# Block merges of a chunked recurrence on one engine, a new block layout, and a new instruction order

## The chip, the cores and the metric

One core of a Trainium2 chip runs the kernel. The time is device microseconds (us) of one execution. A core has a matrix engine (TensorE, PE in the profile, with its weight loads as PEld), VectorE (DVE), ScalarE (ACT) and GpSimd (POOL); SyncE (SP) issues most of the DMA transfers. Each engine takes its instructions in the order in which the program lists them, and waits where an operand is not there yet.

## The reference

Part one is a linear recurrence over 768 steps for 4 batches and 8 heads with a 40x40 state; part two is a two-layer mixer on its output.

```python
for t in range(768):                                   # state: [4, 8, 40, 40]
    y[:, :, t] = einsum('bhd,bhde->bhe', r[t], state)
    Sa = einsum('bhde,bhe->bhd', state, a[t])
    state = state * w[t][:, :, None, :] - einsum('bhd,bhe->bhde', Sa, b[t])
    state = state + einsum('bhd,bhe->bhde', v[t], k[t])
x = y.transpose(0, 2, 1, 3).reshape(4, 768, 320)
h = maximum(x.transpose(0, 2, 1) @ w_tok1, 0) @ w_tok2  # 768 -> 256 -> 768
u = x + h.transpose(0, 2, 1)
out = u + maximum(u @ w_ch1, 0) @ w_ch2                 # 320 -> 1536 -> 320
```

## The kernel before

The 768 steps of a batch are cut into 12 chunks of 64, so there are 48 chunks (number 0 to 47), taken one after the other: the state passes from chunk to chunk in the chain (`t_chain`, the lines from 1236 on). What a chunk needs besides the state is prepared ahead. Sixteen chunks are a *unit* (three units); `t_prep` takes a unit in four quarters of 128 partitions each: running products of w by a scan (L550), a reciprocal (L564, L583), then RC, a product of eight steps, each on the result of the one before (L577 for the first, L579 for seven more; `prc` is the name of its tile in the odd quarters of unit 0), and two multiplies of the inputs by RC (L422, `pin<-pin,RC`) and one by the products themselves. The results go to DRAM (`sKB`, `sA`, `sP`) and come back chunk by chunk. P is the part of that product by which a chunk's y is multiplied in the end.

Inside a chunk of 64 steps the rank-one terms are coupled by a triangular 64x64 system. Its two 32x32 diagonal blocks are inverted for a *set* of eight chunks at once on VectorE (`t_solve`, six sets): ScalarE or VectorE copies the blocks out of TensorE's result into the tile `Dg` (`e3` in `t_a`, L886 and L890), one transpose turns them (L930, into `DT`), 15 pairs of multiply and reduce invert the 16x16 blocks (L952, L954), and *left* and *right* steps (L967 and L969, L988, L980 and L983) merge 16-blocks into 32-blocks. Two more transposes give TBt and TBn (L1008, L1013). For the first `pem` sets the left and right steps are left out, and TensorE merges the 16-blocks instead, chunk pair by chunk pair: `merge`, with 64 matmuls of 32x32 (L1102), a half copy (L1109) and two adds (L1114) on VectorE for each chunk, and an additional copy `noff` (L875) of the off-diagonal block. From TBt and TBn, `t_b` makes the 64-blocks (TensorE L1155, L1180, L1205), and the chain of a chunk can begin: `pq` (L1271), a copy (L1286), a second product (L1291), and RM on VectorE (L1327 in the first chunks, later L1321), which marks a chunk's start in what follows.

`t_y` multiplies the chunk pair's y by P: P comes by a DMA on SyncE's queue (L1435, `UB<-sP`), the multiply is L1437. The mixer (`t_mlp`) runs batch by batch beside the recurrence of the next batches, and after chunk 47 alone for the last batch; its weights are split in two parts ahead (`t_piece`, tiles `cv_t`, `cv_c`).

The order of all this isn't written by hand. Each stage is a Python generator that yields its instructions; a `Planner` builds the list of each engine from them at compile time, by ranks (when a piece is due) and by assumed costs. All ranks and choices stand in one table of numbers, `K`. Where the planner expects TensorE to stand still, it puts in *filler* matmuls (L409, 128x192 on constants, with a result that nobody reads), from `fill` us on.

Of the kernel before, what the change touches and what calls it, by code (L numbers as in the profile page):

```python
# [26 lines left out]
K = dict(mgs=0, mgl=0, lat=[200.0, 150.0, 145.0, 90.0], aff=[1.42609, 1.1641], affx=[1.5189, 1.1228], aff_g=8.09865,  # L27
         sets=[8, 8, 8, 8, 8, 8], atn=6, kbp=2, ld=6.86684, ldk=0.75246, v=10.13755, vg='APD', tbd_early=39.49165,
         tbd=[['DP', 'AD', 'DP', 'AP'], ['DA', 'PD', 'PD', 'P']], alt_c=1, slack=-25499.24339, evm=32.40994,
         slack_c=220.65128, p_rc=[1, 0, 1], p_a=[0, 0, 0], p_k=[0, 0, 0], solve=[3.58374, 3.18399, 3.06635, -7.44996,  # L30
         3.58843, -8.1416], solve_span=16.42651, atomic=0, a=11.69153, a_span=3.813, b=1.3893, chain=0.36562,
         evac=12.39546, y=-0.34229, utr=-4.08779, pem=1, mrg=2.46972, ea=7.45819, prp=15, psp=10, w=3, c=2, m=2,
         warm=0, fill=6, fill_cols=9045.48295, prep=[-24.70881, 2.11658, 24.34216], prep_step=[2.30023, -1.32604,
         0.5187], p_wg=[1, 3], p_big=[2], mlp=[11.83919, 26.61413, 33.74329, 43.48104], mlp_span=[14.28446, 11.00328,
         12.73272, 15.91023], conv_t=4.92844, conv_t_span=1.14477, conv_c=3.69813, conv_c_span=11.72512, conv_after=4,
         e_k=-29.62124, e_a=-24.52265, e_s=-2.04992, e_x=-24.28583, e_l=-10.57978)
# [1988 lines left out]
```

## Time and profile before

| | us |
|---|---|
| median of 3 runs (863.05 to 863.92) | 863.5 |
| the profiled execution | 866.96 |
| its span in the trace | 865.3 |
| TensorE busy | 785.6 (91%) |
| VectorE busy | 603.2 (70%) |
| ScalarE busy | 411.0 (47%) |
| GpSimd busy | 188.5 (22%) |

The busy shares are averages over three stages: up to about 115 us there is preparation only and no chunk runs; then the chunks run, with more and more of the mixer beside them; from about 790 us on only the last batch's mixer is left. TensorE's share holds 84.5 us of filler matmuls. A time in the trace is counted from the span's start.

### The profile page before, as it was taken

Reading aid. Unit: us, or ns where it says so; the run is one execution under the profiler, and the core shown is the slowest. Engines: PE = TensorE matmul, PEld = TensorE weight load, DVE = VectorE, ACT = ScalarE, POOL = GpSimd, SP = SyncE. Lnnn points to the kernel's source line nnn. Section 1 sums busy time; section 2 is a strip of 40 time slices with the busy share of each in tenths; the row PEclk is TensorE's granted clock in tenths of the full one; section 3 lists DMA queues with packets and bytes.
Section 4 is the critical chain, followed back from the end, with each engine's and each line's share of the span. In section 5 each row is a group of like instructions: output and inputs, shape, how many; then the busy total and the mean of one; then the engine's idle time right before and its main releaser. Section 6 shows DMA issues by size and latency. Waiting matters only on the chain.

```text
span 865.3 us, 31442 instructions
## 1 busy us (share of the span) xinstructions
PE 785.6 (91%) x13365; PEld 689.9 (80%) x13365; DVE 603.2 (70%) x1450; ACT 411.0 (47%) x1136; POOL 188.5 (22%) x314
## 2 busy tenths in 40 slices
PE   5798898888987979897999999999999999999997
PEld 4697786777876867786787988888888888989997
DVE  5657489999889969899663799438975444535332
ACT  2444365457767645447554655454453333423111
POOL 7500222234436123214420110111120001000000
PEclk7889788778978869998899999999999999999999
DMA  8489157998879866866958754743745445335341
GB/s 321 167 160 231 46 175 219 239 261 196 243 185 268 289 168 205 225 142 170 242 143 254 185 147 114 180 94 86 222 127 165 128 115 152 116 108 188 101 147 49
DMA packets 191379, 150.86 MB, mean 174 GB/s; under 512 B 147200, under 2 KB 167424, under 8 KB 188160
## 3 DMA queue, kind: packets, MB, share of 16 engines
q1 hardware_dynamic: 184896, 101.59, 45.6%
q0 software_dynamic: 6336, 47.19, 17.0%
q8 instruction: 107, 1.75, 0.9%
q14 instruction: 40, 0.33, 0.1%
HBM read 114.34 MB, written 34.41 MB: 172 GB/s over the span
## 4 chain that ended last, share of the span: by engine, by line
PE 47%; DVE 14%; issue 11%; DMA 9%; ACT 3%; POOL 1%; SPq 0%; ACTq 0%; POOLq 0%; DVEq 0%
PE m L1673 14%; PE m L1783 10%; DMA cv_c<-in_moe_w_ch_dram 3%; PE ph L1205 3%; PE yb L409 2%; DMA wg_t<-sT 2%; PE pq L1291 2%; DMA sG<-cv_c 2%; PE pq L1271 2%; PE pq L1296 2%; PE yb L1412 2%; PE px L845 1%; PE pU L298 1%; PE pt L1180 1%; DMA UB<-sP 1%
## 5 line engine op out<-in xcount | busy, mean ns | idle before, releaser
L1783 PE MATMUL m<-ut,wg_c 128*128 128x384 f32 x768 | 164.3, 351 | 0.6 <-DVE hd L1796 0.6
L1673 PE MATMUL m<-wg_c,hd 128*128 128x320 f32 x864 | 150.2, 318 | 1.9 <-DVE hd L1796 1.9
L1673 PEld LDWEIGHTS m<-wg_c,hd 128*128 128x128 f32 x864 | 129.8, 189 | 6.5 <-DVE hd L1796 3.6
L1783 PEld LDWEIGHTS m<-ut,wg_c 128*128 128x128 f32 x768 | 130.6, 190 | 5.5 <-DVE hd L1796 0.8
L1794 ACT ACTIVATE hd<-m 128x384 fp32r<-128x384 f32 x96 | 47.2, 491 | 136.5 <-PE m L1783 135.4
L1824 DVE TENSOR_TENSOR x<-m,x 128x320 f32<-128x320 f32 x96 | 46.8, 488 | 65.0 <-PE m L1673 64.6
L1796 DVE SCALAR_TENSOR_TENSOR hd<-m,hd 128x384 fp32r<-128x384 f32 x96 | 53.3, 555 | 50.4 <-ACT hd L1794 49.7
L409 PE MATMUL yb<-ident 128*128 128x192 bf16 x664 | 84.5, 272 | 3.0 <-POOL ident masks.py:199 1.7
L409 PEld LDWEIGHTS <-ident 128*128 128x128 bf16 x664 | 61.8, 108 | 15.1 <-issue 6.8
L422 POOL TENSOR_TENSOR cv_c<-cv_c 128x384 f32<-128x384 f32 (+3 forms) x48 | 49.0, 1021 | 83.1 <-DVE cv_c L1506 31.8
L886 ACT ACTIVATE Dg<-px 128x128 f32<-128x128 f32 (+1 forms) x135 | 52.9, 392 | 29.6 <-PE px L845 19.5
L1146 POOL COPY TBD<-TBt 32x256 f32<-32x256 f32 x43 | 31.3, 729 | 117.8 <-PE ph L1205 66.7
L1386 ACT COPY STs<-pU 40x160 f32<-40x160 f32 x88 | 25.0, 284 | 65.9 <-PE pU L298 64.6
L1608 POOL DMA_DIRECT2D wg_c<-sG x32 | 17.8, 557 | 166.9 <-PE m L1783 72.3
L1412 PE MATMUL yb<-KB,RM 128*64 128x40 f32 x768 | 39.4, 226 | 1.2 <-issue 1.2
L1271 PE MATMUL pq<-RV 40*64 40x64 f32 x768 | 37.6, 233 | 2.3 <-issue 1.5
L1305 POOL TENSOR_TENSOR RM<-UB,upp 64x128 f32<-64x128 f32 x30 | 15.6, 526 | 107.4 <-ACT UB L1286 98.0
L1271 PEld LDWEIGHTS pq<-RV 40*64 40x64 f32 x768 | 30.7, 143 | 10.0 <-issue 7.5
L1291 PE MATMUL pq<-UB 104*64 104x104 f32 x240 | 33.8, 311 | 3.6 <-ACT UB L1286 3.6
L1286 ACT COPY UB<-pq 104x256 f32<-104x256 f32 x96 | 31.5, 378 | 11.8 <-PE pq L1271 11.2
L298 PE MATMUL pU<-id,UB 40*40 40x40 f32 x352 | 24.7, 205 | 13.5 <-DVE UB L1371 8.8
L1412 PEld LDWEIGHTS yb<-KB,RM 128*64 128x64 f32 x768 | 34.1, 141 | 3.0 <-issue 2.7
(200 smaller groups left out, 1755.4 us busy)
## 6 DMA issues: line engine op xcount, KB each, us to landing
wg_c<-sG POOLq DMA_DIRECT2D x16, 1152.0 KB, 6.4
wg_c<-sG POOLq DMA_DIRECT2D x16, 960.0 KB, 5.4
pin<-in_wakb_dram SPq DMA_DIRECT2D x12, 960.0 KB
wg_t<-sT POOLq DMA_DIRECT2D x8, 1280.0 KB, 7.0
RV<-in_rvt_dram SPq DMA_DIRECT2D x48, 208.0 KB
sKB<-pin SPq DMA_DIRECT2D x12, 640.0 KB
KB<-sKB SPq DMA_DIRECT2D x48, 160.0 KB
KBp<-sKB SPq DMA_DIRECT2D x40, 160.0 KB
```

The source lines that it names most:

```text
L298: nc.tensor.matmul(out_, lhsT=in_, rhs=idn, start=True, stop=True, is_transpose=True)
L409: nc.tensor.matmul(yb[:, 320:512], lhsT=zf[:, 0:128], rhs=zf[:, 0:192], start=True, stop=True)
L422: return [(e, Port(60 + f * n / 0.96 if e == "DVE" else 140 + 2.24 * n), lambda e=e: engines[e].tensor_tensor(out=out_(), in0=a_(), in1=b_ ...
L886: act_ = ("ACT", 395, lambda: nc.scalar.activation(out=o_, in_=i_, func=AF.Copy, scale=-1.0))
L1271: nc.tensor.matmul(pqs[g][z][0][c0:c1, j, D:DP], lhsT=l_, rhs=rb[z * 64:z * 64 + D, j, :], start=True, stop=True)
L1291: nc.tensor.matmul(d["pq"][64:128, j, :], lhsT=hu[:, gi, j, :], rhs=hv(G)[:, j, :], start=True, stop=True)
L1412: nc.tensor.matmul(py[g - 1][z * 64:z * 64 + 64, h, :], lhsT=rms[g - 1 + z][:, h, :], rhs=o["kb"][:, h, :], start=h == 2 * j, stop=False)
L1673: nc.tensor.matmul(d[key], lhsT=lhs(i, a_), rhs=rhs(i, b_), start=i == 0 and j == 0, stop=i == n - 1 and j == 2)
L1783: nc.tensor.matmul(pt, lhsT=mm_[q][0], rhs=mm_[q][1], start=q == 0, stop=q == len(mm_) - 1)
L1794: nc.scalar.activation(out=hid[key][:, 0], in_=pt, func=AF.Relu)
L1796: now = yield [("DVE", dve(384), lambda: nc.vector.scalar_tensor_tensor(out=hid[key][:, 1], in0=pt, scalar=0.0, in1=hid[key][:, 0].bitcast ...
L1824: now = yield [("DVE", dve(320), lambda: tt(out=x()[:, i], in0=d[("c2", g, i)], in1=x()[:, i], op=ALU.add))]
```

## The change

Five things change, all in one edit of the table and a few lines of code.

1. `pem` goes from 1 to 0: the 16-blocks of all six sets, the first included, are merged by the left and right steps on VectorE. The `merge` work (512 small matmuls, 8 half copies, 16 adds, 8 `noff` copies) is no longer in the program.
2. `Dg` is stored chunk by chunk, so that the copies into it write whole rows, and the transpose L930 reads it with a stride.
3. The load of P is a small generator of its own, `pload`, with a due time ahead of the y matmuls; `t_y` is started by the main loop.
4. RC of unit 0 may go to VectorE or GpSimd (`p_rc` 2 for 1: the planner takes the one that is free by its count); RC of unit 1 goes to GpSimd (1 for 0).
5. All ranks of `K` and a few assumed costs have other numbers, and filler matmuls may stand from 2 us on, not 6. This gives another order on every engine. The program has 1217 filler matmuls, where it had 664.

Of the table, these two lines show the kind (the rest is numbers in the same manner):

```diff
-         slack_c=220.65128, p_rc=[1, 0, 1], p_a=[0, 0, 0], p_k=[0, 0, 0], solve=[3.58374, 3.18399, 3.06635, -7.44996,
+         slack_c=253.99266, p_rc=[2, 1, 1], p_a=[0, 0, 0], p_k=[0, 0, 0], solve=[5.34224, 2.30103, 3.06635, -9.75835,
-         evac=12.39546, y=-0.34229, utr=-4.08779, pem=1, mrg=2.46972, ea=7.45819, prp=15, psp=10, w=3, c=2, m=2,
+         evac=11.65466, y=0.17357, utr=-1.79783, pem=0, mrg=0.91121, ea=7.77917, prp=14, psp=10, w=3, c=2, m=2,
```

The code:

```diff
 # t_a, e3
-            o_, i_ = Dg[sl, :, ci * NP:(ci + 1) * NP].rearrange("p s n -> p n s"), pxb[sl, :, c0:c0 + L]
+            o_, i_ = Dg[sl, ci * NP:(ci + 1) * NP, :], pxb[sl, :, c0:c0 + L]
 # t_solve, first
-                nc.vector.transpose(out=d["DT"][:, 0:1024].rearrange("p (t s) -> p s t", t=L), in_=Dg)
+                nc.vector.transpose(out=d["DT"][:, 0:1024].rearrange("p (t s) -> p s t", t=L), in_=Dg.rearrange("p n s -> p s n"))
 # t_y
+        direct = bi == B - 1
+        pt = Pv_
+        p_ev = Event()
+
+        def pload():
+            yield g - K["y"] - K["y_ld"]
+            yield R_p
+            now = yield [("SP", (640.0, 960.0, 1024), lambda: nc.sync.dma_start(out=pt, in_=sP[u][:, cu - 1:cu + 1].rearrange("h c t e -> (c t) h e")))]
+            P.set(p_ev, now)
+        now = yield None
+        P.spawn(pload(), g - K["y"], now)
+        for z in range(2):
             for e in range(2):
                 yield rm_done[g - z][e]
...
-        direct = bi == B - 1
-        if not direct:
-            yield R_p
-        elif c == 1:
+        if direct and c == 1:
...
-        yield [("SP", (640.0, 960.0, 1024), lambda: nc.sync.dma_start(out=pt, in_=sP[u][:, cu - 1:cu + 1].rearrange("h c t e -> (c t) h e")))]
+        yield p_ev
         P.hold = 1e12
         now = yield [("DVE", dve(320), lambda: tt(out=to, in0=py[g - 1], in1=pt, op=ALU.mult))]
...
-            P.rel(R_p, now)
+        P.rel(R_p, now)
```

What it does to the order, at four places.

VectorE, the end of the first set's solve, before: the last pair of the 16-blocks, the two transposes, two products `AT` of chunks further on, and the half copies (`ET`) and adds of the merges on TensorE (`pm`).

```order
L952 TENSOR_TENSOR tmp_15_1160<-Tl_114,DT_954 128x450
L954 TENSOR_REDUCE Tl_114<-tmp_15_1160 128x2x15
L1008 STREAM_TRANSPOSE TBt_1183<-Tl_114 128x1024
L1013 STREAM_TRANSPOSE TBn_1210<-Tl_114 128x1024
L871 TENSOR_TENSOR AT_126<-px_1157,low_90 128x4x64
L871 TENSOR_TENSOR AT_126<-px_1158,low_91 128x4x64
L1109 TENSOR_SCALAR ET_135<-pm_1235,half 128x4x16
L1114 TENSOR_TENSOR TBt_1183<-pm_1235,TBt_1183 128x4x16
L1114 TENSOR_TENSOR TBn_1210<-pm_1235,TBn_1210 128x4x16
```

VectorE at the same place, now: after the last pair the left steps follow (`tmp_x`, `DT`) ...

```order
L954 TENSOR_REDUCE Tl_114<-tmp_14_1189 128x2x14
L952 TENSOR_TENSOR tmp_15_1207<-Tl_114,DT_1004 128x450
L954 TENSOR_REDUCE Tl_114<-tmp_15_1207 128x2x15
L967 TENSOR_TENSOR tmp_x_0_1232<-DT_1004,Tl_114 128x512
L969 TENSOR_REDUCE DT_1004<-tmp_x_0_1232 128x8x4
L967 TENSOR_TENSOR tmp_x_8_1255<-DT_1004,Tl_114 128x512
L969 TENSOR_REDUCE DT_1004<-tmp_x_8_1255 128x8x4
```

So the merge has moved from TensorE's results into VectorE's own list, ahead of the transposes, and these come 51 rows below that pair. Right ahead of them stand the last of nine steps on converted weights (`cv_t`), and behind them the multiply by RC of unit 1's second quarter, its scan, and the first copy `TBD` for a chunk's 64-blocks:

```order
L1515 SCALAR_TENSOR_TENSOR cv_t_0_128_1500<-cv_t_0_128_1500 128x384
L1515 SCALAR_TENSOR_TENSOR cv_t_0_0_1506<-cv_t_0_0_1506 128x384
L422 TENSOR_TENSOR cv_t_0_0_1506<-cv_t_0_0_1506 128x384
L1008 STREAM_TRANSPOSE TBt_1768<-Tl_114 128x1024
L1013 STREAM_TRANSPOSE TBn_1795<-Tl_114 128x1024
L422 TENSOR_TENSOR pin_1_1200<-pin_1_1200,RC_1_1663 128x640 x2
L544 COPY D_110<-CP_1_1595 128x40
L550 SCALAR_TENSOR_TENSOR CP_2_1851<-pin_2_993,D_110 128x680
L422 TENSOR_TENSOR pin_1_1200<-pin_1_1200 128x640
L1186 COPY TBD_156<-pt_1861 32x4x32
```

The copy `TBD`, too, now stands behind all this. Between the two places stand the left and right steps, mixed with the scans and reciprocals of unit 1's first two quarters and the multiplies of the first; these stood behind the merges before.

TensorE, ahead of the first chunk's 64-blocks (`pe`), before: the last matmuls of a merge, then `pe`.

```order
L298 MATMUL pk_0_1525<-ident,KBp_118 104x128 x4
L1102 MATMUL pm_1497<-ET_135,TBn_1210 32x32 x16
L1102 MATMUL pm_1497<-TBn_1210,ET_135 32x32 x16
L1155 MATMUL pe_1524<-TBt_1183,N_0_758 32x32
L1155 MATMUL pe_1524<-TBt_1183,N_1_770 32x32
```

TensorE now, at the same `pe` (`ident` and `yb` are a filler matmul's operands):

```order
L409 LDWEIGHTS ident
L409 MATMUL yb<-ident 128x192
L1155 MATMUL pe_1797<-TBt_1768,N_0_837 32x32
L1155 MATMUL pe_1797<-TBt_1768,N_1_844 32x32
L1155 MATMUL pe_1797<-TBt_1768,N_0_837 32x32
```

The merges are gone, and `pe` follows on filler matmuls, 172 in one piece. From the last `px` of the first set's chunks to this `pe` there are 443 of them in all (188 in the same stretch before).

SyncE's queue, the load of P for the chunk pair 16 and 17, before: it stands behind the two loads of unit 2's last quarter (`pin_3`) and a store of weights (`sG`).

```order
L509 DMA pin_3_5610<-in_wakb_dram 128x680
L1519 DMA sG_178<-cv_c_2_2_5378 128x384 x2
L509 DMA pin_3_5610<-in_wakb_dram 128x1920
L425 DMA RV_146<-in_rvt_dram 104x512
L1435 DMA UB<-sP_168 128x8x40
L425 DMA RV_147<-in_rvt_dram 104x512
L1057 DMA KB_5700<-sKB_162 128x8x40
L425 DMA W2s_145<-in_vtok_dram 64x320
```

Now (`pin_1` and `pin_2` are that unit's second and third quarter):

```order
L425 DMA W2s_143<-in_vtok_dram 64x320
L425 DMA sKB_163<-pin_1_4839 256x1x640
L425 DMA sA_166<-pin_1_4839 8x8x640 x2
L425 DMA sP_169<-pin_1_4839 128x640
L1406 DMA UB<-sP_168 128x8x40
L1057 DMA KB_5232<-sKB_162 128x8x40
L509 DMA pin_2_5318<-in_wakb_dram 128x680
L509 DMA pin_2_5318<-in_wakb_dram 128x1920
```

The load has moved ahead by a quarter of the unit: it stands behind the stores of the second quarter and ahead of the loads of the third.

## Rows read from the trace of the kernel before

**Rows 1.** The page: its first line, and shares of the chain that ended last.

```profile
span 865.3 us, 31442 instructions
...
PE 47%; DVE 14%; issue 11%; DMA 9%; ACT 3%; POOL 1%; SPq 0%; ACTq 0%; POOLq 0%; DVEq 0%
```

**Rows 2.** Windows: stretch, length, busy us of each engine (instructions), PE clock, DMA share.

```profile
64.40:115.30 50.90, 44.05 (x1043) 38.02 (x1040) 34.85 (x86) 24.11 (x61) 6.75 (x9) 0.87 0.54 146
...
115.30:221.50 106.20, 90.87 (x1973) 78.15 (x1972) 96.33 (x217) 62.86 (x164) 33.33 (x39) 0.81 0.85 222
...
404.00:431.00 27.00, 24.01 (x409) 19.66 (x409) 19.19 (x40) 15.73 (x43) 12.08 (x19) 0.75 0.91 225
...
431.00:790.00 359.00, 350.92 (x5604) 306.94 (x5602) 223.06 (x582) 165.74 (x497) 44.47 (x77) 1.00 0.54 147
```

**Rows 3.** Timeline of VectorE: start, length, line, operation; in brackets idle time before it.

```profile
16.01 1.56 DVE L422 TENSOR_TENSOR pin<-pin,RC 128x640 f32<-128x640 f32 x2 [6.36 <-POOL RC L579]
...
39.00 0.82 DVE L422 TENSOR_TENSOR pin<-pin,prc 128x640 f32<-128x640 f32 x1 [3.81 <-POOL prc L579]
...
64.37 1.97 DVE L930 STREAM_TRANSPOSE DT<-Dg 128x1024 f32<-128x1024 f32 x1 [0.20 <-ACT Dg L886]
...
79.58 1.21 DVE L1013 STREAM_TRANSPOSE TBn<-Tl 128x1024 f32<-128x1024 f32 x1
...
115.28 0.42 DVE L1327 TENSOR_TENSOR RM<-pq,upp 128x256 f32<-128x256 f32 x1
...
221.48 0.42 DVE L1327 TENSOR_TENSOR RM<-pq,upp 128x256 f32<-128x256 f32 x1 [1.31 <-ACT W2s L1337]
```

**Rows 4.** Timeline of GpSimd, 12 to 31 us: RC of the first unit.

```profile
12.76 3.21 POOL L579 TENSOR_TENSOR RC<-RC,pin 128x80 f32<-128x80 f32 x7
...
25.39 5.75 POOL L579 TENSOR_TENSOR RC<-RC,pin 128x80 f32<-128x80 f32 x7
```

**Rows 5.** VectorE by line: busy us, mean ns of one, then idle us before them.

```profile
L967 DVE TENSOR_TENSOR tmp_x<-DT,Tl 128x512 f32<-128x512 f32 (+2 forms) x30 | 21.3, 712 | 0.6
...
L980 DVE TENSOR_TENSOR tmp_y<-DT 128x512 f32<-128x512 f32 (+2 forms) x30 | 18.0, 600 | 0.5
...
L983 DVE TENSOR_REDUCE Tl<-tmp_y 128x32 f32<-128x384 f32 (+3 forms) x30 | 17.9, 595 | 0.6
...
L969 DVE TENSOR_REDUCE DT<-tmp_x 128x32 f32<-128x512 f32 (+3 forms) x30 | 17.8, 592 | 0.5
...
L579 DVE TENSOR_TENSOR RC<-RC,pin 128x80 f32<-128x80 f32 x28 | 11.3, 404 | 0.1
...
L550 DVE TENSOR_TENSOR_SCAN CP<-pin,D 128x680 f32<-128x680 f32 x10 | 16.4, 1643 | 1.6 <-DMA pin<-in_wakb_dram 1.3
...
L422 DVE TENSOR_TENSOR pin<-pin,RC 128x640 f32<-128x640 f32 x20 | 16.1, 819 | 7.2 <-POOL RC L579 7.0
...
L890 DVE TENSOR_SCALAR Dg<-px 32x128 f32<-32x128 f32 x9 | 3.7, 406 | 1.5 <-ACT Dg L886 1.4
...
L875 DVE TENSOR_SCALAR N<-px 128x128 f32<-128x128 f32 x8 | 2.3, 287 | 0.8 <-PE px L761 0.8
```

**Rows 6.** Timeline of TensorE between 66 and 102 us.

```profile
67.22 0.60 PE L298 MATMUL pk<-ident,KBp 128*104 128x128 f32 x4
...
67.66 2.97 PE L409 MATMUL yb<-ident 128*128 128x192 bf16 x34
...
94.39 5.01 PE L409 MATMUL yb<-ident 128*128 128x192 bf16 x36
...
101.40 0.21 PE L1155 MATMUL pe<-TBt,N 32*32 32x32 f32 x1
```

**Rows 7.** Windows for line L409 alone: the filler matmuls, from chunk 0 to 8.

```profile
115.30:221.50 106.20, 13.52 (x99) 9.53 (x99) 0.81 0.85 222
```

**Rows 8.** VectorE by line: the multiply with P.

```profile
L1437 DVE TENSOR_TENSOR UB<-yb,UB 128x320 f32<-128x320 f32 x18 | 8.7, 482 | 9.7 <-DMA KB<-sKB 5.0 <-DMA UB<-sP 4.5
...
L1437 DVE TENSOR_TENSOR x<-yb,UB 128x320 f32<-128x320 f32 x6 | 2.9, 490 | 5.8 <-DMA UB<-sP 5.8
```

More of the change, by code (lines that the diff above doesn't have):

```diff
@@ L24 @@
 LAT = {"PE": 190.0, "ACT": 210.0, "DVE": 130.0, "POOL": 150.0, "SP": 1000.0, "SWD": 1100.0}
[L27 to L36 removed]
+K = dict(mgs=0, mgl=0, lat=[200.0, 150.0, 145.0, 90.0], aff=[1.78829, 1.1641], affx=[1.45405, 1.4136], aff_g=9.17793,
+         sets=[8, 8, 8, 8, 8, 8], atn=6, kbp=2, ld=6.28181, ldk=0.00651, v=7.41899, vg='DAP', tbd_early=37.54021,
+         tbd=[['DP', 'AD', 'DP', 'PA'], ['DA', 'A', 'PD', 'PA']], alt_c=1, slack=-26924.458, evm=27.39028,
+         slack_c=253.99266, p_rc=[2, 1, 1], p_a=[0, 0, 0], p_k=[0, 0, 0], solve=[5.34224, 2.30103, 3.06635, -9.75835,
+         3.58843, -15.141], solve_span=15.10055, atomic=0, a=11.69153, a_span=3.89302, b=1.3893, chain=0.2847,
+         evac=11.65466, y=0.17357, utr=-1.79783, pem=0, mrg=0.91121, ea=7.77917, prp=14, psp=10, w=3, c=2, m=2,
+         warm=0, fill=2, fill_cols=9045.48295, prep=[-21.43568, -0.09764, 24.34216], prep_step=[2.31794, -1.32604,
+         0.31432], p_wg=[1, 3], p_big=[2], mlp=[11.83919, 26.61413, 33.74329, 43.92168], mlp_span=[14.28446, 11.00328,
+         12.73272, 15.91023], conv_t=5.1196, conv_t_span=-1.53208, conv_c=3.86709, conv_c_span=11.83065, conv_after=2,
+         y_ld=0.77206, e_k=-29.43179, e_a=-22.97064, e_s=-12.37189, e_x=-24.15062, e_l=-16.89014)
 class Port(float):
@@ L552, in scan @@
                         data1=D1.rearrange("p e t -> p (e t)"), initial=0.0, op0=ALU.mult, op1=ALU.add)
-                now = yield [("DVE", Port(120), carry), ("DVE", 1490, scan)]
+                now = yield [("DVE", Port(250), carry), ("DVE", 1560, scan)]
                 P.set(scan_ev[q], now)
@@ L559, in comp @@
                 cq = ce[:, q * n8:(q + 1) * n8]
-                yield [("ACT", 245, lambda: nc.scalar.activation(out=cq, in_=CPv[:, :, 7], func=AF.Square))]
+                yield [("ACT", 330, lambda: nc.scalar.activation(out=cq, in_=CPv[:, :, 7], func=AF.Square))]
                 def rec():
@@ L928, in first @@
                 d["DT"] = ap_.tile([128, 1056], F32, tag="t4", name=f"DT{i}", bufs=4)
-                nc.vector.transpose(out=d["DT"][:, 0:1024].rearrange("p (t s) -> p s t", t=L), in_=Dg)
-            now = yield [("DVE", 1810, first)]
+                nc.vector.transpose(out=d["DT"][:, 0:1024].rearrange("p (t s) -> p s t", t=L), in_=Dg.rearrange("p n s -> p s n"))
+            now = yield [("DVE", 2300, first)]
             P.set(Dg_free[i + 1], now)
@@ L1340, in body @@
             now = yield None
-            if c % 2 and gi:
-                P.spawn(t_y(g), g - K["y"], now)
             if last:
@@ L1878, in tile_kernel @@
                 P.spawn(t_b(g), g - K["b"])
+            else:
+                P.spawn(t_y(g), g - K["y"])
         for gi in range(2):
```

11 lines of the change are left out of this document (5 added, 6 removed).

## The prediction

> **What bounds the kernel now.** I read the page first: 865.3 us of span, and in the chain that ended last 47% TensorE, 14% VectorE, 11% issue and 9% DMA [rows 1]. Such shares mix stages, so the next view is the windows [rows 2]. The reader is to see two regimes. From 115.3 to 221.5 us VectorE is busy 96.33 of 106.2 us, TensorE 90.87, of which 13.52 are fillers [rows 2, 7]: VectorE is the engine that nothing can be taken from. From 431 to 790 TensorE is busy 350.92 of 359 us at a clock of 1.00, VectorE only 223.06: there the matrix work sets the pace. Before 115.3 no chunk runs; VectorE is busy 34.85 of the last 50.9 us of it. The third view is the timeline of VectorE [rows 3], for the points where stages begin: the first transpose at 64.37, TBn of the first set ending at 80.8, the first RM (chunk 0) at 115.28, RM of chunk 8 at 221.48. Chunk 8 is the first that needs the second set, whose solve shares VectorE with chunks 0 to 7. So an earlier end comes from an earlier chunk 8, if TensorE can use the time further on.
>
> The sum is made in the profiled execution, 866.96 us (its span and 1.66 around it). It lies 3.46 above the median of 863.5; I lay the difference on the median.
>
> **Up to the first transpose.** In the first quarter VectorE waits 6.36 us for RC, in the fourth 3.81 for prc [rows 3]. GpSimd's seven steps begin at 12.76 and take 3.21, beside a busy VectorE 5.75 [rows 4]. In the new order four of the first quarter's eight steps are VectorE's, then three GpSimd's, then one VectorE's. GpSimd still gets there at 12.76 only, so the gain is the half of its steps, 2 us. In the fourth quarter all eight are VectorE's: 8 x 0.404 = 3.2 us [rows 5] in place of GpSimd's chain and the wait; I count 3 us for that and for the second quarter, whose chain is shared now. Then the copies: eight `noff` copies go, 8 x 0.287 = 2.3 us by the N copies [rows 5]. VectorE's copy into Dg, a quarter of the N copy's partitions and the same row length, takes 406 ns against N's 287 [rows 5]; Dg is written with a stride and N in a row, so I take 287 for the new copies. VectorE has twelve of them (nine before), four on all partitions: 12 x 0.287 = 3.4 against 9 x 0.406 = 3.7, and ScalarE's, of which VectorE waits for several, shrink as well; 1.3 us in all. Sum 8.6, so the transpose starts near 56 instead of 64.37. Ends: nothing gained (64.4), and 10.2, the two whole waits, with it.
>
> **The first set's solve.** From the transpose to the end of TBn before: 16.4 us [rows 3]. To that come left and right: five sets took 21.3 + 18.0 + 17.9 + 17.8 = 75.0 us [rows 5], 15.0 a set. Among them stand 23 other rows: two scans (2 x 1.64), three multiplies (3 x 0.82) [rows 5], nine weight steps and some ten small ones, together 19 to 20 at 0.44, the mean of the window (96.33 us in 217) [rows 2]: 14.5 in all. TBn ends at 56 + 16.4 + 15.0 + 14.5 = 102. Instructions that stood behind the merges are ahead of TBt now, and a late one (RC of unit 1 comes from GpSimd, the weights by DMA) holds TBt, with every chunk behind it. The merges on TensorE, which go, ended so that `pe` ran at 101.40 [rows 6]. TensorE's queue has to be there as well: 443 fillers at 2.97 / 34 = 0.087 us [rows 6] are 38.7 us, twelve groups of small transposes 12 x 0.60 = 7.2 [rows 6], four groups of px a little more; begun at some 53 us (the last px of the set, an estimate: it has to be copied before the transpose at 56), that ends near 103. I take `pe` at 103.
>
> Dg is read with a stride by the transpose now. L930 with a strided side took 1.97 us, L1013 with none 1.21 [rows 3]. A second strided side costs between nothing and another 0.76; I take 0.75, since one side did: 1.5 us for the two transposes ahead of the first RM. The Trainium skill ("SBUF — State Buffer", section "Door 1: The DMA port swizzle") speaks against this part of the change: accesses that go to a new 16-byte line each time pay a penalty, so that a stride beyond four fp32 is not free. The rows with one strided side agree with that; by it the new transpose is dearer on both sides, and by a rule that only the worse side counts the sum would be 1.5 us smaller.
>
> From `pe` to the first RM it took 115.28 - 101.40 = 13.9 us before. So the first RM comes at 103 + 13.9 + 1.5 = 118.4, say 119: **3.7 us later** than before.
>
> **Chunk 0 to 8.** Counted in the two orders with the rows' durations, VectorE has 106.1 us of work between these RMs before, which is the stretch's length of 106.2, and 81.1 after. What goes: 24 steps of RC of unit 1, to GpSimd, 24 x 0.404 = 9.7; three scans (4.9) and eight multiplies (8 x 0.82 = 6.6), done ahead of chunk 0 now; reciprocals and small steps of the same, and the last half copies and adds of the merges, 17 at about 0.35, 6; against that 2 us of weight steps come in. The stretch can't be shorter than 81.1, if VectorE stays as full as before. TensorE without fillers needs 90.87 - 13.52 = 77.3. The DMA share is 0.85 [rows 2], so 0.85 x 106.2 = 90.3 us in which the DMA engines are at work; if all of that had to pass in the stretch, it would be the bound. Some of it is weights, which can come later. I take 87: **19.2 us less**.
>
> **From chunk 8 on.** The counted work of VectorE is the same from 8 to 16 (98.3 and 98.0) and 16 to 24 (98.3 and 96.1), and the mixer's matmuls stand beside the same chunks from 33 on. The shift is carried, with one exception: around chunks 22 and 23 the new order has 98 fillers more, 98 x 0.087 = 8.6 us in which the planner saw TensorE without work, and there (404 to 431) the clock was 0.75 and the DMA share 0.91 [rows 2]. TensorE had 3 us idle there before as well. I take 3 us given back, ends 0 and 8.6.
>
> P ahead of time: VectorE waited 4.5 + 5.8 = 10.3 us for `UB<-sP` [rows 8]; another 5.0 is for KB and stays. Most of it lies where TensorE is the bound, so its gain is between 0 and 10.3; I take 0.5, since VectorE is busy there for 223.06 of 359 us only [rows 2] and a short wait has room. Moved ahead on SyncE's queue, the load passes the loads of a unit's next quarter, so these are later by one issue; that quarter is needed many chunks on.
>
> Clock: it was 0.87 and 0.81 in the first two windows and 1.00 later [rows 2]. More fillers may raise it; 36 fillers took 5.01 us at the low level and 34 took 2.97 [rows 6]. I count nothing for it.
>
> Sum: +3.7 - 19.2 + 3 - 0.5 = **-13.0**, so 853.9 for the profiled execution, and 850.5 us.
>
> **Rivals.**
> *More is gained*: VectorE stays full (81.1) and nothing is given back: +3.7 - 25.1 - 1.5 = -22.9, 840.6. For it: the stretch before was as long as its counted work. Against it: the DMA share of 0.85.
> *Given back*: DMA bounds the stretch (90.3) and the 8.6 us at chunks 22 and 23 are paid in full: +3.7 - 15.9 + 8.6 - 0.5 = -4.1, 859.4. For it: 0.91 at 404 to 431. Against it: weight steps stand earlier in VectorE's order now, as the nine ahead of TBt.
> *RC is paid twice*: GpSimd's steps for unit 1 hold VectorE up. GpSimd's own seven steps went from 3.21 to 5.75 beside a busy VectorE [rows 4], so somebody pays. 32 steps at 3.21 / 7 = 0.46 are 14.7 us; half of it on VectorE is 7.4: -5.6, 857.9. The Trainium skill ("SBUF — State Buffer", section "Who interferes with whom") has this as an exclusive lock: a VectorE instruction with two inputs in SBUF and a GpSimd one that reads SBUF exclude each other, and the loser blocks. The two rows agree for GpSimd's side; none shown here tells what VectorE loses.
> *Slower: the fillers hold back the first `pe`.* All 443 stand ahead of it in TensorE's queue. At the low clock's 5.01 / 36 = 0.139 us they take 61.6, not 38.7; `pe` comes at 53 + 61.6 + 11 = 126, the first RM at 141: +26 - 19.2 + 3 - 0.5 = +9.3, 872.8. It decides from a first RM later than 132, since the 19.2 and what follows give 13 beyond 119. A late RC or weight step ahead of TBt would act at the same place. For it: the fillers of before had low clocks just there (94.39) [rows 6]. Against it: that many fillers leave TensorE few gaps.
>
> **How the numbers follow.** Forecast 0.55, with its own range of 844 to 857 (200 or 209 for chunk 8 in place of 206, with the ends of the copies and of P); more 0.07; given back 0.12; RC paid twice 0.10; slower 0.16. About 0.2% (1.7 us) is what a measurement can tell from no change. Slower holds 0.16; within 0.2% are the upper edges of the rivals that end just below, 0.06; faster the rest, 0.78. The range is 840 to 865: below it is half of the larger gain, above it the slower case.
>
> **What would show it.** The transpose L930 near 56, TBn's end near 102 with no wait ahead of L1008, the first RM near 119 and that of chunk 8 near 206; new transposes of up to 2.7 us; no line L1102; VectorE's idle on `UB<-sP` gone; fillers with little idle behind them at chunks 22 and 23. It is wrong if the first RM comes after 132, if VectorE between chunks 0 and 8 is much below 90% busy, or if the distance won at chunk 8 is gone by chunk 24.

## The result

The changed kernel took 838.34 us in the median of four runs (831.59 to 846.63), the kernel before 863.27: 24.9 us less, where 13.0 were forecast, and below the range of 840 to 865. The ratio is 0.969 (0.963 to 0.975); it leaves out the slowest of the four runs, 846.63 us, which is the profiled one, so that a second profile of the same program, of 840.11 us (**a_same**, under the experiments), is read beside it. The profiled execution is 20.3 us shorter than that of before (866.96), the second 26.9.

The page of the kernel after, its first line and the shares of the chain that ended last, answer to [rows 1]:

```profile
span 844.9 us, 31014 instructions
...
PE 52%; issue 13%; DVE 12%; DMA 4%; SPq 1%; ACT 1%; POOL 1%; DVEq 0%; POOLq 0%; ACTq 0%
```

TensorE's share is larger, VectorE's and the DMA's smaller. The windows of the kernel after, cut at its own points (first transpose, first RM, RM of chunk 8, ScalarE's copy L1286 of chunks 24 and 47), with the columns of [rows 2] (busy us of TensorE, its weight loads, VectorE, ScalarE and GpSimd, each with its instructions; then the granted clock, the DMA share and GB/s):

```profile
56.30:117.95 61.65, 55.70 (x951) 50.72 (x949) 58.07 (x110) 31.54 (x80) 18.67 (x35) 1.00 0.68 189
117.95:202.17 84.22, 74.11 (x1607) 63.70 (x1608) 76.43 (x169) 53.51 (x149) 29.20 (x36) 0.98 0.87 209
202.17:408.40 206.23, 191.53 (x3542) 162.42 (x3542) 177.55 (x415) 119.04 (x339) 68.41 (x107) 0.92 0.79 221
408.40:745.50 337.10, 329.25 (x5380) 287.12 (x5381) 216.26 (x563) 156.65 (x470) 41.27 (x72) 0.99 0.55 148
745.50:844.80 99.30, 93.95 (x674) 88.86 (x674) 38.92 (x85) 21.62 (x58) 5.28 (x10) 0.99 0.38 122
```

The second profile of the changed kernel, a_same, at its own points:

```profile
57.91:119.50 61.59, 55.56 (x951) 50.66 (x948) 58.17 (x110) 31.46 (x80) 18.64 (x35) 1.00 0.68 190
119.50:202.68 83.18, 75.43 (x1609) 65.05 (x1610) 76.61 (x168) 53.67 (x149) 29.40 (x36) 0.96 0.89 215
202.68:402.76 200.08, 186.42 (x3540) 158.42 (x3539) 178.03 (x415) 119.08 (x339) 68.57 (x107) 0.95 0.80 226
402.76:739.16 336.40, 328.20 (x5380) 285.78 (x5381) 215.91 (x563) 156.64 (x471) 41.22 (x72) 0.99 0.55 148
739.16:838.40 99.24, 93.93 (x674) 88.84 (x674) 38.90 (x85) 21.62 (x58) 5.28 (x10) 1.00 0.38 122
```

The kernel before at the same points of its work, for the last three:

```profile
221.50:430.70 209.20, 182.53 (x3381) 155.97 (x3380) 182.92 (x424) 121.81 (x339) 71.75 (x105) 0.87 0.79 213
430.70:764.00 333.30, 326.70 (x5384) 284.78 (x5385) 212.07 (x553) 157.14 (x468) 42.82 (x74) 0.99 0.55 148
764.00:865.20 101.20, 94.74 (x677) 89.26 (x677) 38.89 (x85) 21.61 (x58) 5.34 (x10) 0.99 0.38 122
```

Against the profile of before, in us:

| stretch | profiled | second profile |
|---|---|---|
| first RM | 2.7 later | 4.2 later |
| from there to chunk 8 | 22.0 less | 23.0 less |
| chunk 8 to 24 | 3.0 less | 9.2 less |
| chunk 24 to 47 | 3.8 more | 3.1 more |
| behind chunk 47 | 1.9 less | 2.0 less |

The larger part lies where the prediction put it, before chunk 8. The two profiles of one program agree within 2 us in every stretch but one, chunk 8 to 24, where they differ by 6.2. Before chunk 0 VectorE is busy 58.07 of 61.65 us, where it had 34.85 of 50.9: the work that was between chunks 0 and 8 fills the idle time of the first solve. From the first transpose to chunk 8 VectorE has about as much to do as before (134.5 us and 131.2), in 145.9 us for 157.1.

VectorE's timeline after, at the points of [rows 3] (columns as there):

```profile
14.03 1.56 DVE L422 TENSOR_TENSOR pin<-pin,RC 128x640 f32<-128x640 f32 x2
...
56.32 1.94 DVE L930 STREAM_TRANSPOSE DT<-Dg 128x1024 f32<-128x1024 f32 x1
...
99.75 1.96 DVE L1008 STREAM_TRANSPOSE TBt<-Tl 128x1024 f32<-128x1024 f32 x1
101.64 1.19 DVE L1013 STREAM_TRANSPOSE TBn<-Tl 128x1024 f32<-128x1024 f32 x1
...
117.95 0.76 DVE L1327 TENSOR_TENSOR RM<-pq,upp 128x256 f32<-128x256 f32 x2
...
202.17 0.42 DVE L1327 TENSOR_TENSOR RM<-pq,upp 128x256 f32<-128x256 f32 x1 [0.21 <-ACT W2s L1337]
```

The transpose comes at 56.3 (forecast 56), TBn ends at 102.8 (102), the first RM is at 117.95 (119), chunk 8's at 202.17 (206).

By line after, for VectorE, in answer to [rows 5] and [rows 8] (busy us, mean ns of one, idle us before them):

```profile
L930 DVE STREAM_TRANSPOSE DT<-Dg 128x1024 f32<-128x1024 f32 x6 | 11.9, 1978 | 0.1
L890 DVE TENSOR_SCALAR Dg<-px 32x128 f32<-32x128 f32 x8 | 2.3, 282 | 1.7 <-ACT Dg L886 1.6
L1443 DVE TENSOR_TENSOR UB<-yb,UB 128x320 f32<-128x320 f32 x18 | 8.8, 487 | 8.7 <-PE yb L1426 8.5
L1443 DVE TENSOR_TENSOR x<-yb,UB 128x320 f32<-128x320 f32 x6 | 2.9, 491 | 2.8 <-PE yb L1426 2.7
L1515 DVE SCALAR_TENSOR_TENSOR cv_t<-cv_t 128x384 f32<-128x384 uint32 x8 | 7.5, 951 | 0.0
```

The copy into Dg fell from 406 to 282 ns. The transpose that now reads with a stride too takes 1978 ns, as the one at 64.37 did before (1.97 us). The multiply by P (L1443 now) no longer waits for P; it waits 11.2 us for TensorE's y instead. The weight steps `cv_t` are dearer (951 ns on average): before they took 653,

```profile
L1509 DVE SCALAR_TENSOR_TENSOR cv_t<-cv_t 128x384 f32<-128x384 uint32 x8 | 5.2, 653 | 0.0
```

### The profile page after: what moved, and what is told of

The parts are those of the page before. It is cut to its first block, busy times and chain, and to the rows that moved or that the text cites. A ratio compares the mean times of both kernels' runs of the same rounds, so it can differ in the third digit from the quotient of the medians.

```text
span 844.9 us, 31014 instructions
## 1 busy us (share of the span) xinstructions
PE 793.6 (94%) x13150; PEld 699.2 (83%) x13150; DVE 606.0 (72%) x1434; ACT 404.4 (48%) x1144; POOL 185.6 (22%) x321
## 4 chain that ended last, share of the span: by engine, by line
PE 52%; issue 13%; DVE 12%; DMA 4%; SPq 1%; ACT 1%; POOL 1%; DVEq 0%; POOLq 0%; ACTq 0%
PE m L1679 14%; PE m L1789 12%; PE yb L409 4%; PE pq L1271 2%; PE pq L1296 2%; PE ph L1205 2%; DMA cv_c<-in_moe_w_ch_dram 2%; PE pq L1291 2%; PE yb L1422 2%; PE pU L298 1%; PE px L845 1%; PE pk L298 1%; PE pe L1155 1%; PE yb L1426 1%; PE pS L1356 1%
## 5 line engine op out<-in xcount | busy, mean ns | idle before, releaser
L409 PE MATMUL yb<-ident 128*128 128x192 bf16 x1217 | 133.6, 257 | 2.8 <-POOL ident masks.py:199 1.7
L409 PEld LDWEIGHTS <-ident 128*128 128x128 bf16 x1217 | 105.5, 102 | 15.8 <-issue 5.6
L422 POOL TENSOR_TENSOR cv_c<-cv_c 128x384 f32<-128x384 f32 (+3 forms) x45 | 44.6, 993 | 76.5 <-ACT cv_c L1513 28.7
L886 ACT ACTIVATE Dg<-px 128x128 f32<-128x128 f32 x132 | 35.6, 270 | 18.3 <-PE px L845 7.8
L1146 POOL COPY TBD<-TBt 32x256 f32<-32x256 f32 x36 | 25.2, 700 | 66.8 <-PE ph L1205 55.3
L1271 PEld LDWEIGHTS pq<-RV 40*64 40x64 f32 x768 | 29.5, 141 | 10.2 <-issue 7.0
L1286 ACT COPY UB<-pq 104x256 f32<-104x256 f32 x96 | 31.4, 378 | 12.7 <-PE pq L1271 11.9
L1426 PE MATMUL yb<-STs,RV 104*64 104x80 f32 x384 | 35.2, 253 | 0.0
L1271 PE MATMUL pq<-RV,STs 40*40 40x64 f32 x768 | 35.0, 228 | 0.1
```

The lines of the kernel that those rows point to most:

```text
L409: nc.tensor.matmul(yb[:, 320:512], lhsT=zf[:, 0:128], rhs=zf[:, 0:192], start=True, stop=True)
L422: return [(e, Port(60 + f * n / 0.96 if e == "DVE" else 140 + 2.24 * n), lambda e=e: engines[e].tensor_tensor(out=out_(), in0=a_(), in1=b_ ...
L886: act_ = ("ACT", 250, lambda: nc.scalar.activation(out=o_, in_=i_, func=AF.Copy, scale=-1.0))
L1271: nc.tensor.matmul(pqs[g][z][0][c0:c1, j, D:DP], lhsT=l_, rhs=rb[z * 64:z * 64 + D, j, :], start=True, stop=True)
L1426: nc.tensor.matmul(py[g - 1][z * 64:z * 64 + 64, 2 * j:2 * j + 2, :].rearrange("p h e -> p (h e)"), lhsT=o["rb"][:, j, :], rhs=o["sp"][:, ...
```

## The experiments

Each was timed in five rounds beside the kernel before, whose runs there lie between 853.0 and 870.7 us. "Order kept" means that only what is sent was changed, not the planner's order. Two theories stood at first for the larger part of the gain: S, VectorE's work moved ahead of chunk 0; C, the clock, since the mean granted clock of TensorE rose from 0.922 to 0.971 in the profiled executions, and the prediction had counted nothing for it.

### The clock (order kept)

**a_same**, the changed kernel again.

> The changed kernel itself once more, as the control of this group. Its four times so far lie between 831.6 and 846.6 us, with a mean granted clock of TensorE between 0.971 and 0.989, the slowest at the lowest clock; the kernel before gave 861.4 to 863.9. Theory S (structure: VectorE's work moved ahead of chunk 0, carried to the end) expects a median near 838 and a spread that has nothing to do with the clock. Theory C (clock: the gain is time that TensorE no longer spends at the low clock) expects the time of a run to fall by about 1 us for each us that its clock's shortfall, (1 - clock) x span, is smaller.

Measured: 839.4 us (827.8 to 841.9), ratio 0.971 (0.964 to 0.977). C's mark is there within one kernel: of its ten runs so far the longest (846.63, clock 0.971) is 18.8 us above the shortest (827.81, clock 0.988), and its shortfall of the clock 14.6 us larger. Which of the two brings the other, this run can't tell.

**a_nofill** and **a_half**: in the changed kernel

```diff
     def filler():
-        nc.tensor.matmul(yb[:, 320:512], ...)
+        return                        # a_half: only every second call is left out
```

> The changed kernel with none of its 1217 filler matmuls sent; the order of everything else on every engine is the same. Theory S: first RM at 118 +- 3 us, RM of chunk 8 at 202 +- 4, 834 to 844 us in all, since fillers only fill gaps. Theory C: the clock's shortfall goes back to that of the kernel before or beyond (67 us there, 25 in the profiled run of the changed one), and the time to 855 to 875 us; the first transpose of the solve then comes several us after 56.

> The changed kernel with every second filler matmul sent, 608, about as many as the kernel before has (664); order otherwise the same. Theory S: 834 to 844 us. Theory C: between the control and the kernel without fillers, 845 to 860 us.

Measured: 840.1 us (838.9 to 843.0), 0.978 (0.974 to 0.982), at a clock of 0.893; and 837.1 us (830.6 to 840.1), 0.974 (0.969 to 0.978), at 0.950. The windows of a_nofill at the same points of its work:

```profile
56.78:118.64 61.86, 29.46 (x509) 22.86 (x507) 58.11 (x110) 31.76 (x80) 17.98 (x35) 0.52 0.74 200
118.64:206.84 88.20, 71.32 (x1459) 61.74 (x1460) 76.30 (x168) 53.51 (x149) 29.05 (x35) 0.81 0.85 200
206.84:412.60 205.76, 181.00 (x3272) 151.84 (x3272) 177.25 (x415) 119.18 (x339) 69.43 (x107) 0.82 0.78 221
412.60:744.80 332.20, 324.22 (x5326) 282.63 (x5327) 216.02 (x563) 156.54 (x470) 41.66 (x72) 0.99 0.56 149
744.80:839.10 94.30, 87.43 (x599) 85.07 (x599) 38.82 (x85) 21.58 (x58) 5.29 (x10) 0.99 0.40 129
```

From the first transpose to the first RM the clock is 0.52 (at 1.2 GHz nearly throughout, half of 2.4) and TensorE is busy 29.5 of 61.9 us; yet the first RM comes at 118.64, between those of the two profiles with all fillers (117.95 and 119.50), since VectorE has its 58.11 us in any case. Against a_same the fillers are worth 5.0 us from chunk 0 to 8 (83.2 for 88.2) and 5.7 to chunk 24; from there to 47 they cost 4.2 and behind it 4.9. On balance nothing: C falls as the cause of the gain, for this order. The six runs scatter less without fillers: 838.9 to 843.0, and 827.8 to 841.9 with them.

**b_double**: in the kernel before, `for _ in range(2):` ahead of the filler matmul.

> The kernel before with each of its 664 fillers sent twice, 1328, about as many as the changed kernel has; order otherwise the same. Theory S: 863 us or up to 10 more, since the additional ones only stand ahead of useful matmuls. Theory C: the clock's shortfall falls from 67 to some 30 to 40 us and the time to 840 to 855.

Measured: 893.4 us (888.9 to 903.5), 1.038 (1.033 to 1.043), at a clock of 0.932. The first RM came at 126.2, and the stretch behind chunk 47 took 106.8 us for 101.3. More fillers on TensorE are no remedy; both theories expected less harm.

### The parts of the change (planned anew)

**b_pem0** is the kernel before with `pem=0`; **a_pem1** the changed one with `pem=1`; **a_rcold** the changed one with `p_rc=[1, 0, 1]`; **b_code** the changed code with the table of before.

> The kernel before with pem 0 alone: all six sets merged on VectorE, every other number and line as before (the planner makes its order anew). Counted by the mean row durations of before, VectorE has 87.6 us of work ahead of the first RM (80.8 before, 105.7 in the changed kernel) and 106.4 from there to the RM of chunk 8 (106.1 and 81.1). Theory S (what counts is how much of VectorE's work stands ahead of chunk 0, and how much between chunks 0 and 8): the first RM 5 to 12 us later than 115, no shorter stretch, so 865 to 875 us. Rival M (the merge on VectorE is itself the gain, since TensorE and VectorE no longer wait for each other in the merges): 840 to 855.

> The changed kernel with pem 1: the first set's merges go back to TensorE, all other numbers as changed. VectorE's counted work is 78.5 us ahead of the first RM and 101.6 from there to chunk 8. Theory S: the stretch from the first RM to that of chunk 8 is 100 to 106 us, as before; the first RM is some 8 us earlier than in the changed kernel, so chunk 8 comes 10 to 15 later, and 848 to 856 us in all. Rival M: 855 to 865, all of the gain gone.

> The changed kernel with RC as before: unit 0's on GpSimd alone, unit 1's on VectorE. VectorE's counted work is 108.2 us ahead of the first RM and 85.0 from there to chunk 8. Theory S: the first RM 3 to 8 us later (VectorE waits for GpSimd's RC as before, 4 to 5 us, and has 2.5 us more to do), chunk 8 another 4 later, 843 to 852 us. If GpSimd's RC holds VectorE up by the shared port, as one rival of the prediction has it, part of that comes back: 838 to 842.

> The changed code with the table of before (pem 1, RC as before, old ranks, fillers from 6 us on; P's load with no lead of its own): what is left of the change is the layout of Dg, the load of P by a generator of its own and the assumed costs. VectorE's counted work is 81.4 us ahead of the first RM and 103.7 to chunk 8. Theory S: 856 to 862 us, 1 to 3 of it from the copies into Dg ahead of the first solve. The prediction's terms for the copies and the loads of P give together 1 to 4.

Measured: b_pem0 859.7 us, 0.996 (0.992 to 0.999); a_pem1 849.1, 0.985 (0.979 to 0.990); a_rcold 834.6, 0.967 (0.963 to 0.972); b_code 845.3, 0.979 (0.973 to 0.986). In the whole time only a_pem1 is where S put it; M, which expected 855 to 865 there and 840 to 855 for b_pem0, misses both. The merges on VectorE alone give 0.4%, RC as before costs nothing in all, and the code without the table already gives 2%. The points of the traces, one execution each (the points of chunks 22, 24 and 47 are ScalarE's copy L1286; some of these runs come further on, and b_code's took 836.4 us where its median is 845.3):

| us | first RM | RM of chunk 8 | chunk 22 | chunk 24 | chunk 47 | end |
|---|---|---|---|---|---|---|
| before | 115.28 | 221.48 | 403.89 | 430.73 | 763.98 | 865.25 |
| after | 117.95 | 202.17 | 376.54 | 408.42 | 745.52 | 844.93 |
| a_same | 119.50 | 202.68 | 371.75 | 402.76 | 739.16 | 838.40 |
| a_nofill | 118.64 | 206.84 | 378.35 | 412.60 | 744.80 | 839.19 |
| b_pem0 | 106.29 | 209.16 | 400.73 | 423.75 | 759.14 | 859.85 |
| a_pem1 | 95.55 | 209.10 | 375.41 | 415.99 | 742.21 | 842.40 |
| a_rcold | 124.75 | 214.35 | 387.38 | 419.42 | 737.74 | 837.19 |
| b_code | 104.37 | 205.07 | 371.52 | 402.88 | 735.06 | 834.58 |
| b_dg | 109.66 | 215.06 | 393.65 | 421.05 | 752.54 | 853.85 |
| b_nop | 114.44 | 218.87 | 393.68 | 420.74 | 753.84 | 854.25 |
| a_rc201 | 115.07 | 202.09 | 370.16 | 400.09 | 723.47 | 823.40 |

S by counted work holds up to chunk 8 for a_rcold: first RM 5.2 later than in a_same (3 to 8 expected), chunk 8 11.7 later. For a_pem1 it has the direction alone: the first RM 24 us earlier than in a_same (8 expected), 113.6 us from there to chunk 8 (100 to 106). It fails for b_pem0, whose first RM is 9.0 earlier than before where S had it 5 to 12 later, and for b_code: 103.7 us of VectorE's work between chunks 0 and 8, measured 100.7, but the first RM 10.9 earlier with 0.6 more counted ahead of it. And an early chunk 8 isn't always carried: b_pem0 has it 12.3 earlier than before and only 3.2 of that at chunk 22; a_rcold has it 11.7 later than a_same and ends earlier, since its stretch from chunk 24 to 47 takes 318.3 us for 336.4. Three parts of b_code remained.

**b_dg** is the kernel before with the two lines of Dg's layout (order kept); **b_pload** with the generator for P alone; **b_cost** with the assumed costs alone; **a_dgold** the changed kernel with the two Dg lines as before (order kept).

> The kernel before with Dg stored by chunk and read by the transpose with a stride, and nothing else; the order is that of before on every engine. The run with the changed code and the old table came out at 845 us, 15 below what counted work of VectorE let expect, so one of three things in it must be worth that: the layout of Dg (theory D), the load of P ahead of time (theory P), or the order that the planner makes from other assumed costs (theory O). D expects 845 to 852 here, with the first transpose 4 us earlier and the gain growing set by set. P and O expect 858 to 862.

> The kernel before with the load of P in a generator of its own and t_y started by the main loop, and nothing else but the order that the planner makes from that. P expects 845 to 852, with no wait of VectorE for UB<-sP. D expects 858 to 862. O expects anything between, by chance of the order: the counted work of VectorE between the first RM and that of chunk 8 is 107.9 us, 1.8 more than before.

> The kernel before with the changed kernel's assumed costs (scan, ScalarE's square, RC, reciprocal, copies into Dg, first transpose) and nothing else: all instructions are those of before, the order is planned with other numbers. O expects 845 to 852. D and P expect 858 to 866; by VectorE's counted work (86.5 us ahead of the first RM, 107.9 from there to chunk 8) rather the slower end.

> The changed kernel with Dg stored as before (strided copies, contiguous read of the transpose), order as in the changed kernel. D expects 848 to 858. P and O expect 839 to 843: the 132 copies of ScalarE are 0.1 us longer each, hidden beside VectorE, and the first transpose comes 3 to 4 us later.

Measured: b_dg 860.1 us, 1.000 (0.997 to 1.003); b_pload 846.8, 0.983 (0.978 to 0.987); b_cost 863.1, 1.003 (1.000 to 1.006); a_dgold 840.8, 0.972 (0.966 to 0.978). The layout and the costs are worth nothing by themselves; D and O fall. The layout does what it should at its place. The timeline of VectorE in b_dg, to be held against the transpose in [rows 3]:

```profile
60.07 1.99 DVE L930 STREAM_TRANSPOSE DT<-Dg 128x1024 f32<-128x1024 f32 x1
```

4.3 us earlier than before, and in the median nothing at the end. In the one trace the lead is kept to the end (853.85 for 865.25), but that execution took 855.55 us, the median is 860.1: where the other runs lose it is not shown. What is left is P.

### P, and the order

**b_nop**: the kernel before, order kept, with the load sent for the first pair alone (`... if g == 1 else None`).

> The kernel before without 23 of its 24 loads of P (only the first pair's is sent; the later pairs multiply by what is in the tile, so that part of the output is not the reference's). The order of everything else is that of before on every engine. The load of P by a generator of its own took 861 to 847 us. If the waits of VectorE for UB<-sP are what that is worth (theory W: an in-order engine that waits 10 us loses them), this gives 846 to 852. If it is the order that the planner makes when P does not hold it up (theory O2), this stays at 857 to 861.

Measured: 852.2 us (847.1 to 856.0), 0.990 (0.984 to 0.995). Its multiply by P, against [rows 8]:

```profile
L1437 DVE TENSOR_TENSOR UB<-yb,UB 128x320 f32<-128x320 f32 x18 | 8.6, 480 | 0.2
L1437 DVE TENSOR_TENSOR x<-yb,UB 128x320 f32<-128x320 f32 x6 | 2.9, 483 | 0.0
```

The 15.5 us of waits of VectorE are gone, those for KB too, and 9 us (4 to 14) come off the time, at the edge of what W expected (846 to 852). But the places do not fit W as a rule. In the kernel before one wait of 3.15 us stands between chunks 18 and 19, and the others, 9.6 us, between chunk 24 and 47 (the longest is the second line), with 2.6 behind it:

```profile
354.64 0.49 DVE L1437 TENSOR_TENSOR UB<-yb,UB 128x320 f32<-128x320 f32 x1 [3.15 <-DMA UB<-sP]
...
465.45 0.49 DVE L1437 TENSOR_TENSOR UB<-yb,UB 128x320 f32<-128x320 f32 x1 [5.00 <-DMA KB<-sKB]
```

The windows of b_nop from chunk 8 to 24 and to 47:

```profile
218.87:420.74 201.87, 179.67 (x3381) 153.46 (x3380) 182.24 (x424) 121.82 (x339) 71.52 (x105) 0.88 0.77 215
420.74:753.84 333.10, 327.25 (x5384) 285.24 (x5384) 212.00 (x553) 157.10 (x468) 42.80 (x74) 0.99 0.51 141
```

From chunk 24 to 47, where 9.6 us of waits went, the stretch takes 333.1 us as before (333.3): there they were not on the path. From 8 to 24, where VectorE is as busy as TensorE (87%), it is 7.4 shorter (4.9 of it between chunks 18 and 19), and 2.6 are gained ahead of chunk 8, where no such wait stood. b_nop also takes 23 transfers off the DMA engines and off SyncE's queue; what of the 9 us is theirs is not told apart.

**b_plate** is b_pload, and **a_plate** the changed kernel, with the load held back until the y matmuls:

```diff
             yield g - K["y"] - K["y_ld"]
+            for z in range(2):
+                for e in range(2):
+                    yield y_done[g - z][e]
             yield R_p
```

**a_rc201** is the changed kernel with `p_rc=[2, 0, 1]`.

> The generator for P's load and t_y started by the main loop, but the load issued only when the pair's y matmuls are planned to be done, as in the kernel before. VectorE's order is that of before up to about chunk 40. W: 858 to 863, the waits for UB<-sP are back. O2: also 858 to 863, since the plan is the old one; with a gain of over 5 us it would be the start of t_y by the main loop.

> The changed kernel with P's load issued only when the pair's y matmuls are planned to be done. W: VectorE waits for UB<-sP again, some 10 us, and 848 to 854. O2: 840 to 856, according to what the plan loses. If the gains of the parts do not add, because another part already gives the time that P's load gives: 839 to 843.

> The changed kernel with unit 0's RC on either engine as changed and unit 1's RC on VectorE as before (p_rc 2, 0, 1). With both as before it took 834.6 us, not slower than the changed kernel. If unit 1's RC on GpSimd is what costs (VectorE held up by the port, transposes TBt of later sets late), 832 to 837 here, the best so far. If unit 0's is, 838 to 842.

Measured: b_plate 866.0 us, 1.004 (1.000 to 1.008): held back, the generator gives nothing (its order is nearly that of before), so b_pload's gain is that of the lead and the order planned with it, which these runs don't part. But a_plate took 829.7, 0.965 (0.960 to 0.971), less than the changed kernel and below what any of its theories expected, though VectorE waits for P in it:

```profile
L1446 DVE TENSOR_TENSOR UB<-yb,UB 128x320 f32<-128x320 f32 x18 | 8.7, 486 | 6.6 <-DMA UB<-sP 6.5
L1446 DVE TENSOR_TENSOR x<-yb,UB 128x320 f32<-128x320 f32 x6 | 2.9, 491 | 7.7 <-DMA UB<-sP 7.1 <-DMA out_dram<-x 0.6
```

And a_rc201 took 825.5 (821.2 to 827.8), 0.959 (0.954 to 0.965): the fastest of all, faster than both kernels. Its windows from the first RM to chunk 8, to 24 and to 47:

```profile
115.07:202.09 87.02, 81.96 (x1715) 69.55 (x1705) 76.81 (x174) 53.74 (x150) 27.98 (x31) 0.92 0.80 203
202.09:400.09 198.00, 191.14 (x3629) 165.48 (x3630) 178.44 (x417) 120.29 (x344) 75.49 (x117) 0.99 0.83 232
400.09:723.47 323.38, 320.42 (x5328) 279.01 (x5328) 212.21 (x553) 154.67 (x469) 43.25 (x74) 0.99 0.57 155
```

It reaches chunk 8 when the changed kernel does (a_same 202.68), and gains 2.1 us on a_same up to chunk 24 and 13.0 from there to 47, in stretches in which its edit has no work to move: all 32 steps of unit 1's RC come ahead of chunk 8. That speaks for the order, so two runs drew the order once more without an edit of the work.

**a_jit** is the changed kernel with `lat=[203.0, ...]` for 200.0, **a_jit2** with the scan assumed at 1570 ns for 1560.

> The changed kernel planned with one assumed latency 3 ns longer (203 for 200, of the results of TensorE): the same instructions, in another order. Theory L (the time of a plan scatters by 10 us and more, and edits of a few instructions are read through that scatter): 825 to 850, off the control's 839 by up to 12. Theory N (plans of the same table and code agree): 836 to 842.

> The changed kernel planned with the scan assumed 10 ns longer (1570 for 1560), as a second draw of the order. L: 825 to 850, and not the same as the other draw. N: 836 to 842.

Measured: 843.9 us (840.2 to 850.6), 0.980 (0.975 to 0.984), and 833.1 (828.1 to 836.2), 0.964 (0.960 to 0.968). The intervals don't touch. The work is the same, but with the order the planner also draws other fillers (1283 and 1237, for 1217) and puts 7 and 4 of the steps L1305 on GpSimd in place of VectorE. L holds: a new draw of the plan is worth 5 us to either side here, 10.7 between these two.

## Why the prediction was wrong

The direction was right, and so was the mechanism up to chunk 8: a first RM that comes a little later, and a much shorter stretch from there to chunk 8, since VectorE's work stands ahead of it. The size was half. The step that failed is *From chunk 8 on*: the sum carried the lead of chunk 8 unchanged to chunk 22 and took 2.5 us back behind it (3 given back, 0.5 for P), where the runs show the lead growing, by 8.0 us between chunk 8's RM and chunk 22 in the profiled execution and by 13.3 in the second profile. From chunk 8 to the end the kernel is 1.0 us shorter than before in the first and 8.1 in the second, for 2.5 longer in the sum. The second term that was too small is *chunk 0 to 8*, 19.2 us for 22.0 and 23.0. By the prediction's own steps, in the profiled execution (forecast 853.9, measured 846.6) and the second profile (840.1):

- *Up to the first transpose*: 56.3 and 57.9 for 56. The first multiply by RC starts at 14.03, 2.0 us earlier, as worked out. The sum came out, its parts did not: the layout alone moves the transpose by 4.3 us in b_dg, where 1.3 was charged, and RC as before in a_rcold costs 1.6 to 3.2 (59.50), where 5 were.
- *The strided read*: 0.75 us a transpose was charged, and nothing was to be paid (1978 ns and 1966). The Trainium skill's rule of 16-byte lines ("SBUF — State Buffer", section "Door 1: The DMA port swizzle") agrees with the copies into Dg, 406 to 282 ns once they write in a row; on the transpose, whose other side is strided in any case, a second strided side cost nothing, and there the measurement decides.
- *First set, first RM*: 117.95 and 119.50 for 119, right in size. The rival of the fillers that hold back `pe` is refuted: `pe` began at 101.86, after a wait of 0.35 us for TBt.

```profile
101.86 0.64 PE L1155 MATMUL pe<-TBt,N 32*32 32x32 f32 x32 [0.35 <-DVE TBt L1008]
```

- *Chunk 0 to 8*: 84.2 and 83.2 us for 87. VectorE is busy 76.43 of 84.22, 91%, as before. Its counted work before, 106.1 us, was not its busy time, which is 96.33 in [rows 2]; so 81.1 was no bound either. The bound of 90.3 us of DMA work was none: the share is 0.87 of a shorter stretch, 73 us, so 17 us of transfers simply came at another time.
- *Carried from chunk 8 to 22*: the change was put at nothing, since VectorE's counted work differs by 2.5 us only. Up to chunk 24 it is busy 177.55 and 178.03 us, for 182.92 before, and the wait for P of 3.15 us between chunks 18 and 19 is gone: together some 8 us, for 3.0 and 9.2 measured. That these two are the reason is argued, not shown; no run takes them away alone in the changed order.
- *Given back at chunks 22 and 23*: 3 us were charged, and 5.0 and 4.2 were paid: chunk 22 to 24 takes 31.9 and 31.0 us for 26.8. The fillers planned there were a sign of a real wait and not its cost, since without them (a_nofill) the place takes 34.3.
- *P ahead*: 0.5 us was charged for 10.3 us of waits, with the argument that VectorE is busy only 223 of 359 us there. For that place b_nop bears the argument out: 9.6 us of waits less between chunk 24 and 47 gave 0.2. What the term overlooked is the one wait of 3.15 us ahead of chunk 24. b_nop's 9 us (4 to 14) as a whole are not explained by it, and how much of them is in the changed kernel stays open: a_plate has the waits and isn't slower.
- *From chunk 24 on*: the shift was carried whole, and 3.8 and 3.1 us were lost. That "there the matrix work sets the pace" was too simple. That stretch took 333.3 us before and 323.4 in a_rc201, 318.3 in a_rcold. Without its fillers the changed kernel takes 332.2 there (a_nofill), so the loss goes with the fillers.
- *The clock*: counted as nothing. Against a_nofill the fillers, with the higher clock that they bring, give 10.7 us between chunks 0 and 24 and take 9.1 behind, so on balance nothing was about right.

The difference of the profiled execution from the median was 3.46 us and taken over; after the change it is 8.3 us. That is 4.8 of the 12.2 us between 850.5 and 838.3, a matter of which run was profiled and no step of the kernel. That the gain of the median came out at nearly twice the forecast is therefore in part scatter; the sign of the step that failed is the same in both profiles.

Rivals: *given back* and *slower* are refuted as a whole. *More is gained* (840.6, with a term of 1.5 that is given no source) came nearest in time, but not by its path: the stretch to chunk 8 didn't fall to 81.1, and at chunks 22 and 23 something was given back. *RC is paid twice* isn't settled: GpSimd's seven steps beside a busy VectorE still take 4.03 us or more,

```profile
82.97 4.03 POOL L579 TENSOR_TENSOR RC<-RC,pin 128x80 f32<-128x80 f32 x7
```

but `cv_t` at 951 ns for 653 is little sign of it. Only two of its eight steps stand beside RC on GpSimd, the long ones further on stand beside GpSimd's own `cv_t`, and with RC of unit 1 back on VectorE the eight still take 843 (a_rcold) and 853 ns (a_rc201). VectorE's busy time in the whole program speaks to both sides: 606.5 us in a_same, 600.8 in a_rc201, which has 32 more steps of RC on it, and 608.4 in a_rcold, which has 18 more. Both kernels are no slower than the control (834.6 and 825.5), but one of the two is within the draws of the order (833 to 844), so only a_rc201 goes beyond them, and what it gains lies behind chunk 8. What stays open: a single edit here comes with a new order, whose draws differ by 10.7 us, and the parts (b_pload 14 us against the kernel before, b_code 17, a_pem1 14) do not add up to the whole.

## What to carry to other kernels

Count what an in-order engine has to do between two points where a chain needs it, per engine and by measured durations: that gave chunk 8 within 4 us here and in a_rcold, but b_pem0 and b_code came 17 or more and 14 us earlier than their counts let expect. And a point won in the middle is not yet time won at the end: follow it to the end in the trace, stretch by stretch. Before a wait is charged in full or at nothing, look where each single wait stands, since 9.6 us of them were worth 0.2 us in the stretch that TensorE bounds. Where a planner makes the order, first draw it twice with no edit at all, and read an edit only beyond that scatter, or keep the order and change what is sent.
